# Batch 2's keys and queries by transposing DMA, later loads gated, orders new: attention in front of a two-layer MLP

## The chip, the cores and the metric

The kernel runs on one core of one Trainium2 chip. The metric is the device time of one execution in microseconds. Before the change it is 246.92 us, the median of three executions (246.78 to 246.98).

## The reference

The inputs are `q`, `k`, `v` of shape (8 batches, 8 heads, 576 tokens, 64), a packed query `p` of (8, 8, 32, 64) and two weight matrices. The attention runs twice: `p` attends to `k` and `v`, which gives 32 packed rows for each head, and `q` then attends to these rows, which are its keys and its values at once. The heads laid side by side make 4608 tokens of width 512 for an MLP with 2048 hidden units.

```python
def sm_attn(qq, kk, vv):                      # softmax over the last axis, scale 1/8
    ...
p_packed = sm_attn(p, k, v)
x = sm_attn(q, p_packed, p_packed)            # then (4608, 512)
h = x @ w_in
g = where(h >= 1, h, where(h <= -1, 0, (h + 1) ** 2 / 4))
out = g @ w_out                               # (4608, 512), float32
```

## The kernel before

**Work of one batch.** Loads by POOL's DMA queue bring k, q and v of a batch and cast them to bf16 on the way (`load`, L288). Keys and queries must be turned, so that the head dimension lies over the partitions. There are two ways, chosen in `trans` (L582) for each half (four heads) of k and of q: `by_array` (L400) turns on TensorE, twelve matmuls against an identity into a PSUM tile (`tp`, L409), which ACT or DVE copies to SBUF; `turned` (L574) issues one transposing DMA on SP's queue (L576). Batches from `TURNED` = 3 on take the DMA for all four halves; `BY_DMA` names halves of earlier batches that take it as well, before the change the second query half of batch 2.

Then follow, for each batch: the scores of the packed queries against the keys (`sp`, L436) and their exponential (`ex`, L439); the packed rows and their sums (`pk`, L456 and L462); the second scores (`s`, called s2 in the code, L490), their exponential (`eT`, L500), a matmul with a block of ones that sums and spreads them (`sm`, L505), and the division as an exponential of a logarithm (`ln` L510, `rc` L515, `A` L525). The attention output itself is never formed: the packed rows are multiplied into w_in first (`mp`, L556, copied to `M`), so that the hidden layer is `h = M * A` (L612), 16 tiles of four matmuls for a batch. Each h tile passes ACT (L617), ACT or DVE (L622 or L624) and DVE (L627), which make g, stored turned as `hT`.

**Output tiles.** Two batches are a pair of 1152 tokens and give nine output tiles of 128 tokens, 16 accumulating matmuls each (`o`, L671). A tile is copied to `ob` by ACT or DVE (L352) and stored by SP's DMA queue (L686). The first four tiles of a pair need only the pair's first batch. The first h of a batch needs all of `A`, and so both query halves.

**What sets the order.** Every piece of work is a task with engines, a cost, a key and dependences. `Plan.run` (L135) plays them through with the constants in `C` before anything is emitted, and each engine then takes its instructions in the order that this play gave. At each step an engine takes the task that can start first by the plan, and among those that can start about then the one with the lowest key. The h tiles of batch b have the keys b to b + 15/16, the output matmuls 100 and more, so that these fill what is left; the keys of the attention's units come from the table `KEYS`, one row for each batch. PSUM tiles (`W`, three; `O`, two) are rooms that a task must wait for. While fewer than three output rooms have been taken, matmuls on zeros (L745) fill TensorE's time.

Loads keep the order in which they were added: `FIRST` for batch 0, then `ORDER` (i and o are parts of w_in and w_out; the rest are k, q and v of batch 1, and p), then k, q and v of batches 2 to 7, each released when the batch two before it has used its buffer (L727 to L729). `LATE` names the parts of M of batch 0 that wait for an h tile (L733). SP's queue carries the transposes and the output stores, in the order of the plan.

For SP the plan before has two constants: a transpose holds SP for `xt` = 6.5 us and is landed `xland` = 9.0 us after that.

Of the kernel before, what the change touches and what calls it, by code (L numbers as in the profile page):

```python
# [8 lines left out]

C = dict(load=2.93, half=1.47, w_in=2.54, w_out=2.65, rest=1.25, out=3.2, p=4.3, land=1.13, xt=6.5, xland=9.0,
         tpp=0.06, tp=0.0425, sc=0.0295, pk=1.0, s2=0.245, sm=0.245, M=0.216, h=0.49, o=0.2158, switch=0.11,
         Tca=1.12, Tcd=0.75, ex=0.807, ppo=0.4, ppT=0.41, ppa=0.4, ppd=0.22, rs=0.165,
         eT=0.741, ln=0.651, rc=0.683, A=0.816, Mca=1.014, Mcd=1.223, x=0.651, ta=0.681, td=0.459, hT=0.757, oba=0.586, obd=0.69,
         array=0.2, tell=0.04, feed=0.2567, margin=0.1705, slack=0.8261, wake=1.2, warm=7.0, early=0.06759, wait=0.2014, p4=3.041, bk=0.7609)
OVER = {"ACT": 0.104, "DVE": 0.083}
NW, NO, NX, NB = 3, 2, 5, 6
DW, FILL = 256, 512
PARTS, CUT = 4, 12  # L20

ORDER = 'i0 i1 i2 k1 o0 i3 o1 o2 k0 q0 v q1 o3 p'

UNITS = "kT0 kT1 qT0 qT1 sc0 sc1 pk0 pk1 s20 s21 sm0 sm1 M0 M1 M2 M3".split()
KEYS = [
# [8 lines left out]
SPLIT = ((0, 0), (0, 1))  # L34
LATE = (2, 3)
FIRST = "k0 k1 q0 v0 v1 q10 q11"
IDENT = 3
FLOW = {"q10": 0.75, "q11": 0.75, "k1": 1.54, "q0": 1.82, "in0": 3.55, "in1": 1.89}

TURNED = 3  # L40
BY_DMA = {2: "q1"}


class Task:
# [10 lines left out]
class Plan:  # L55
# [8 lines left out]
    def __init__(self, rooms):  # L64
        self.tasks, self.now, self.mode = [], {e: 0.0 for e in self.ENGINES}, 0
        self.rooms = {nm: [0.0] * n for nm, n in rooms.items()}
        self.count = {nm: 0 for nm in rooms}
        self.now["DMA"] = 3.1
        self.log = []

    def add(self, engines, cost, key, deps, fn, takes=None, readers=0, frees=None, mode=None, slack=None, after=0.0,
# [8 lines left out]
    def ready(self, t, e):  # L80
        at = 0.0
        for d in t.deps:
            if e == "PE":
                lag = 0.0 if d.on == "PE" else C["feed"] + (C["margin"] if t.slack is None else t.slack)
            else:
                lag = C["array"] if d.on == "PE" else C["tell"]
            at = max(at, d.end + lag)
        if t.takes:
            rooms = self.rooms[t.takes]
            for j in range(len(t.readers)):  # L90
                room = rooms[(self.count[t.takes] + j) % len(rooms)]
                if room is None:
                    return None
                at = max(at, room + (C["feed"] if e == "PE" else 0.0))
        return at

    def choose(self, e, given, waiting):
# [23 lines left out]
        for c in sorted(found, key=lambda c: c[1:3]):  # L121
            if c[0] < best[0] + C["wait"] * best[3].cost[e]:
                return c[0], c[3]
# [11 lines left out]
    def run(self, idle):  # L135
        self.line = [t.seq for t in self.tasks if t.engines == ("DMA",)]
        left = {}
        given = {e: [] for e in self.ENGINES}
        for t in self.tasks:
            left[t] = len(t.deps)  # L140
            for d in t.deps:
                d.users.append(t)
            if not t.deps:
                for e in t.engines:
                    given[e].append(t)
        n, fill = len(self.tasks), 0
        while n:
            best = None
            for e in self.ENGINES:
                c = self.choose(e, given, n)  # L150
                if c is not None and (best is None or c[0] < best[0]):
                    best = c[0], e, c[1]
            if self.count["O"] < 3:
                c, step = self.choose("PE", given, n), DW / 2400
                self.now["PE"] = max(self.now["PE"], C["wake"])
                if self.now["PE"] < C["warm"]:
                    step *= 2
                if (c is None or c[0] > self.now["PE"] + step + C["early"]) and best is not None and best[0] > self.now["PE"]:
                    fill += DW
                    self.now["PE"] += step  # L160
                    continue
            assert best is not None
            at, e, t = best
            t.on = e
            cost = t.cost[e]
            if e == "PE" and at < C["warm"]:
                cost *= 2
            if e == "PE" and t.mode is not None and t.mode != self.mode:
                cost += C["switch"]
                self.mode = t.mode  # L170
            self.now[e] = at + (max(cost - OVER[e], 0.02) if e in OVER else cost)
            t.end = at + cost + t.after + (C["land"] if e == "DMA" else 0.0)
            if e == "DMA":
                del self.line[0]
            self.log.append((at, at + cost, e, t))
            if t.takes:
                room = self.rooms[t.takes]
                t.slots = [(self.count[t.takes] + j) % len(room) for j in range(len(t.readers))]
                self.count[t.takes] += len(t.slots)
                for n_, j in zip(t.readers, t.slots):  # L180
                    room[j] = None if n_ else t.end + t.holds
            if t.frees is not None:
                f, j = t.frees
                f.gone[j] = max(f.gone[j], t.end)
                f.readers[j] -= 1
                if f.readers[j] == 0:
                    self.rooms[f.takes][f.slots[j]] = f.gone[j]

            while e == "PE" and fill:
                w = min(fill, FILL)  # L190
                idle(w)
                fill -= w
            if len(t.engines) > 1:
                t.fn(e)
            elif e in ("ACT", "DVE"):
                t.fn(e)
            else:
                t.fn()
            for x in t.engines:
                given[x].remove(t)  # L200
            for u in t.users:
                left[u] -= 1
                if left[u] == 0:
                    for x in u.engines:
                        given[x].append(u)
            n -= 1
# [3 lines left out]
def kernel(  # L210
# [52 lines left out]
    PE, ACT, DVE, DMA, SP = "PE", "ACT", "DVE", "DMA", "SP"  # L263
# [42 lines left out]
    def add_load(nm, b, parts=1, deps=(), cost="load"):  # L306
        for i, hs in enumerate([ALL] if parts == 1 else HS):
            L[nm, b, i] = add(DMA, C[cost] / parts, -1, deps, lambda nm=nm, b=b, hs=hs: load(nm, b, hs))
        if parts == 1:
            L[nm, b, 1] = L[nm, b, 0]  # L310

    def add_weights(which, f):
        if which == "in":
            fn = lambda: nc.gpsimd.dma_start(w_in_sb[:, :, f * FW:(f + 1) * FW], w_in_v[:, :, f * FW:(f + 1) * FW])
        else:
            fn = lambda: nc.gpsimd.dma_start(w_out_sb[:, 4 * f:4 * f + 4], w_out_v[:, 4 * f:4 * f + 4])
        L[which, f] = add(DMA, FLOW.get(which + str(f), C["w_" + which]), -1, (), fn)

# [10 lines left out]
    for n, nm in enumerate(FIRST.split()):  # L329
        i = int(nm[1])  # L330
        L[nm[0], 0, i] = add(DMA, FLOW.get(nm, C["half"] / (len(nm) - 1)), -1, (), (lambda: None) if n else first_loads)
        for j in (range(2) if len(nm) == 2 else (int(nm[2]),)):
            part_of[nm[0], i, j] = L[nm[0], 0, i]
    for nm in ORDER.split():
        if nm == "p":
# [47 lines left out]
    K = {}  # L383
# [6 lines left out]
    def attention(b, key):  # L390
# [197 lines left out]
        q1, qc1 = trans("q", 1, qT, old("s2"))  # L588
        pk, pc, r = zip(*([packed((0,), [e0]), packed((1,), [e1])] if b == 0 or b == 1 and "v0" in ORDER else [packed((0, 1), [e0, e1])] * G))
        K[b, "sc"], K[b, "pk"] = [s0, s1], list(pk)  # L590
# [133 lines left out]
    attention(0, keys[0])  # L724
    for b in range(B):
        if b + 2 < B:
            add_load("k", b + 2, deps=K[b, "kt"])  # L727
            add_load("q", b + 2, deps=K[b, "qt"])
            add_load("v", b + 2, deps=K[b, "pk"])  # L729
        K[b, "h"] = [hidden_tile(b, fi, b + fi / KF) for fi in range(KF)]  # L730
        if b == 0:

            for f in LATE:  # L733
                K[b, "M"][f].deps.append(K[b, "h"][4 * f - 4])
            attention(1, keys[1])
            add_pT(PB, B, C["p4"], [L["p", PB]], False)
        if b % 2 == 1:
            for i in range(NT):
                out_tile(b // 2, i)
        if 0 < b < B - 1:  # L740
            attention(b + 1, keys[b + 1])
# [34 lines left out]
```

## Time and profile before

| | |
|---|---|
| time, median of three | 246.92 us |
| profiled execution | 246.60 us, of which the span from the first to the last instruction is 244.8 us |
| TensorE busy | 238.5 us (97%), its clock granted at 0.997 |
| ACT, DVE, POOL busy | 188.8, 170.4 and 30.4 us |
| software DMA queue (loads) | 18.55 MB, 53.4% of the 16 engines' time |
| SP's DMA queue (stores and transposes) | 15.70 MB, 32.7% |

A row of the profile names the line, the engine (PE is TensorE's matmul, PEld its weight load), the operation and output<-input by the program's names. `x24` is a count. In the table of slices a digit is the busy share of one fortieth of the span in tenths. In the timeline and the chain, the first number is the start in us from the span's beginning, the second the length. Times of matmuls overlap in the timeline, since matmuls are pipelined; the chain counts no time twice. A DMA's row gives the median time from its issue to its landing.

### The profile page before, as it was taken

Reading aid. Unit: us, or ns where it says so; the run is one execution under the profiler, and the core shown is the slowest. Engines: PE = TensorE matmul, PEld = TensorE weight load, DVE = VectorE, ACT = ScalarE, POOL = GpSimd, SP = SyncE. Lnnn points to the kernel's source line nnn. Section 1 sums busy time; section 2 is a strip of 40 time slices with the busy share of each in tenths; the row PEclk is TensorE's granted clock in tenths of the full one; section 3 lists DMA queues with packets and bytes.
Section 4 is the critical chain, followed back from the end, with each engine's and each line's share of the span. In section 5 each row is a group of like instructions: output and inputs, shape, how many; then the busy total and the mean of one; then the engine's idle time right before and its main releaser. Section 6 shows DMA issues by size and latency. Waiting matters only on the chain.

```text
span 244.8 us, 5431 instructions
## 1 busy us (share of the span) xinstructions
PE 238.5 (97%) x2211; PEld 137.9 (56%) x2211; DVE 170.4 (70%) x299; ACT 188.8 (77%) x314; POOL 30.4 (12%) x45
## 2 busy tenths in 40 slices
PE   7998999999999999999999999999999999999994
PEld 2645666566654764566446754675456644664443
DVE  5467994889964798369936996499669936992000
ACT  2378994889948998899888996899889957992110
POOL 8743232010110112002010200000000000000000
PEclk9999999999999999999999999999999999999998
DMA  7999999999999999999969598734170122022222
GB/s 105 198 206 205 207 203 198 202 220 204 210 211 160 245 213 165 138 202 200 208 110 236 78 160 151 162 71 92 43 137 0 46 43 70 19 43 81 54 82 86
DMA packets 55960, 34.65 MB, mean 142 GB/s; under 512 B 28672, under 2 KB 51456, under 8 KB 55936
## 3 DMA queue, kind: packets, MB, share of 16 engines
q0 software_dynamic: 24688, 18.55, 53.4%
q1 hardware_dynamic: 31104, 15.70, 32.7%
q8 instruction: 17, 0.28, 0.4%
q10 hardware_dynamic: 144, 0.07, 0.1%
q14 instruction: 7, 0.06, 0.1%
HBM read 37.22 MB, written 9.44 MB: 191 GB/s over the span
## 4 chain that ended last, share of the span: by engine, by line
PE 90%; DMA 5%; POOL 2%; issue 1%; ACT 0%; ACTq 0%; POOLq 0%
PE o L671 52%; PE h L612 26%; DMA w_in_sb<-in_moe_w_in_dram 5%; PE mp L556 3%; PE pk L456 2%; PE sp L436 2%; PE tp L409 1%; PE sm L505 1%; PE s L490 1%; PE pk L462 1%; POOL q L288 1%; PE o L745 1%; POOL v L288 1%; POOL k L288 0%; PE tpp L366 0%
## 5 line engine op out<-in xcount | busy, mean ns | idle before, releaser
L671 PE MATMUL o<-w_out_sb,hT 128*128 128x512 bf16 (+2 forms) x592 | 140.7, 374 | 0.0
L627 DVE SCALAR_TENSOR_TENSOR hT<-x 128x576 bf16<-128x576 f32 x128 | 90.2, 749 | 0.7
L671 PEld LDWEIGHTS <-hT 128*128 128x128 bf16 x592 | 55.4, 98 | 56.0 <-issue 5.0
L617 ACT ACTIVATE x<-h 128x576 f32<-128x576 f32 x128 | 75.8, 664 | 2.5 <-PE h L612 1.9
L612 PE MATMUL h<-A,M 128*128 128x288 bf16 x512 | 73.9, 286 | 0.3 <-ACT x L617 0.2
L612 PEld LDWEIGHTS <-M 128*128 128x128 bf16 x512 | 49.5, 98 | 21.0 <-issue 1.2
L622 DVE TENSOR_SCALAR x<-x 128x576 f32<-128x576 f32 x73 | 31.4, 459 | 12.5 <-ACT x L617 12.5
L624 ACT ACTIVATE x<-x 128x576 f32<-128x576 f32 x55 | 37.0, 701 | 0.1
L352 ACT COPY ob<-o 128x512 f32<-128x512 f32 (+1 forms) x24 | 14.0, 583 | 21.5 <-PE o L671 21.5
L352 DVE COPY ob<-o 128x512 f32<-128x512 f32 (+1 forms) x9 | 6.0, 670 | 25.4 <-PE o L671 25.3
L352 DVE CAST M<-mp 128x1024 bf16<-128x1024 f32 (+1 forms) x16 | 18.4, 1153 | 7.0 <-PE mp L556 5.2
L525 DVE SCALAR_TENSOR_TENSOR A<-eT,rs,rc 128x576 bf16<-128x576 bf16 (+1 forms) x15 | 11.5, 775 | 14.0 <-ACT rc L515 14.0
L352 ACT CAST M<-mp 128x1024 bf16<-128x1024 f32 (+1 forms) x18 | 16.8, 972 | 5.2 <-PE mp L556 4.8
L439 ACT ACTIVATE ex<-sp 96x768 bf16<-96x768 f32 x16 | 12.8, 807 | 4.8 <-PE sp L436 4.8
L745 PE MATMUL o<-zeros 128*128 128x512 bf16 (+1 forms) x47 | 13.7, 406 | 1.2 <-DVE zeros L276 1.2
L288 POOL DMA_DIRECT2D q<-in_q_dram x11 | 8.3, 757 | 51.6 <-DMA qT<-q 30.7
L510 ACT ACTIVATE ln<-sm 128x576 f32<-128x576 f32 (+1 forms) x17 | 10.6, 621 | 4.1 <-PE sm L505 3.9
L500 ACT ACTIVATE eT<-s,rs 128x576 bf16<-128x576 f32 (+1 forms) x17 | 11.6, 716 | 2.5 <-PE s L490 2.2
L288 POOL DMA_DIRECT2D k<-in_k_dram x10 | 7.5, 747 | 37.3 <-DMA kT<-k 24.9
L515 ACT ACTIVATE rc<-ln 128x576 f32<-128x576 f32 (+1 forms) x17 | 11.1, 655 | 0.5
L556 PE MATMUL mp<-w_in_sb,ppT 64*32 64x512 bf16 x256 | 10.7, 380 | 0.7 <-DMA w_in_sb<-in_moe_w_in_dram 0.7
L288 POOL DMA_DIRECT2D v<-in_v_dram x9 | 7.0, 775 | 16.4 <-PE pk L462 14.3
(48 smaller groups left out, 117.2 us busy)
## 6 DMA issues: line engine op xcount, KB each, us to landing
out_dram<-ob SPq DMA_DIRECT2D x23, 192.0 KB, 3.2
v<-in_v_dram POOLq DMA_DIRECT2D x7, 576.0 KB, 13.5
k<-in_k_dram POOLq DMA_DIRECT2D x6, 576.0 KB, 14.9
q<-in_q_dram POOLq DMA_DIRECT2D x6, 576.0 KB, 12.6
out_dram<-ob SPq DMA_DIRECT2D x22, 128.0 KB, 3.0
w_in_sb<-in_moe_w_in_dram POOLq DMA_DIRECT2D x4, 512.0 KB, 12.7
w_out_sb<-in_moe_w_out_dram POOLq DMA_DIRECT2D x4, 512.0 KB, 17.6
out_dram<-ob SPq DMA_DIRECT2D x22, 64.0 KB, 3.5
```

What stands on the lines that cost most here:

```text
L288: nc.gpsimd.dma_start(tok[nm, b][:, hs].rearrange("p h c d -> p h (c d)"), SRC[nm][b, hs].rearrange("h (p c) d -> p h (c d)", c=NC))
L352: return lambda eng: nc.vector.tensor_copy(out_, in_) if eng == DVE else nc.scalar.copy(out_, in_)
L439: nc.scalar.activation(ex()[:, :, i].rearrange("p e x a n -> p e (x a n)"), box["sp"], AF.Exp, scale=scale)
L500: nc.scalar.activation(box["eT"][:, xs], box["s2"][:, xs, :HALF], AF.Exp, scale=rs()[:, g, 1:])
L556: nc.tensor.matmul(mp[a * NP:(a + 1) * NP, g], pp_of(y, h), w_in_sb[y * D:(y + 1) * D, h // 2, f * FW:(f + 1) * FW], start=True, stop=True)
L612: nc.tensor.matmul(h[:, hf, :HALF], T[b, "M"][:, g, fi * P:(fi + 1) * P], T[b, "A"][:, g, hf], start=(g == 0), stop=(g == G - 1))
L617: nc.scalar.activation(box["x"], box["h"][:, :, :HALF], AF.Prelu, bias=-1.0, alpha=0.5)
L622: nc.vector.tensor_scalar(x, x, 1.0, 0.0, ALU.add, ALU.max)
L624: nc.scalar.activation(x, x, AF.Relu, bias=1.0)
L627: nc.vector.scalar_tensor_tensor(hT[:, fi, col:col + S].rearrange("p (a t) -> p a t", a=2), box["x"], 1.0, box["x"], ALU.min, ALU.mult)
L671: nc.tensor.matmul(box["o", j, part][:, :cs.stop - cs.start], hT[:, fi, i * P:(i + 1) * P], w_out_sb[:, fi, cs], start=(fi == 0 or fi in c ...
L745: plan.run(lambda w: nc.tensor.matmul(o[:, :w], zeros[:, :P], zeros[:, :w], start=True, stop=True))
```

## The change

The change has four parts.

1. `BY_DMA` names all four halves of batch 2, so that both key halves and both query halves are turned by the DMA.
2. The loads of batches 4 to 7 take one more condition, from `PACE`: those of batch b wait for the last h tile of batch b - 3 on TensorE.
3. The plan has another picture of SP's queue: a transpose begins when the one before it has had its turn, takes 6.5 us of turn if the current load ends more than 1 us later and 1.7 us otherwise, and is landed 1.8 us after its turn; a transpose beside loads and a store also push the loads back.
4. `ORDER`, `LATE`, `KEYS`, `FLOW` and several constants of the plan have new values, so that the instructions of every engine stand in a new order.

```diff
-C = dict(load=2.93, half=1.47, w_in=2.54, w_out=2.65, rest=1.25, out=3.2, p=4.3, land=1.13, xt=6.5, xland=9.0,
+C = dict(load=2.93, half=1.45, w_in=2.55, w_out=2.55, rest=1.25, out=3.2, p=4.3, land=1.13, xt=6.5, xs=1.7, xland=1.8, store=0.65,
...
-         array=0.2, tell=0.04, feed=0.2567, margin=0.1705, slack=0.8261, wake=1.2, warm=7.0, early=0.06759, wait=0.2014, p4=3.041, bk=0.7609)
+         array=0.2, tell=0.04, feed=0.1952, margin=0.1875, slack=0.5648, wake=1.2, warm=7.0, early=0.2339, wait=0.02713, p4=13.81, bk=4.48)
...
-ORDER = 'i0 i1 i2 k1 o0 i3 o1 o2 k0 q0 v q1 o3 p'
+ORDER = 'i0 i2 i1 o1 o0 i3 k1 o2 k0 q0 v q1 o3 p'
...
 KEYS = [
...
-    [2.829, 0.713, 2.940, 1.880, 2.243, 2.146, 1.163, 1.347, 1.162, 0.900, 2.620, 1.749, 1.581, 3.049, 2.830, 1.608],
...
+    [1.609, 3.246, 2.961, 2.006, 2.435, 2.926, 3.925, 3.344, 1.643, 2.402, 2.379, 3.963, 1.909, 1.610, 1.771, 4.354],
...
+PACE = {4: (1, 15), 5: (2, 15), 6: (3, 15), 7: (4, 15)}
 SPLIT = ((0, 0), (0, 1))
-LATE = (2, 3)
+LATE = (3,)
...
-FLOW = {"q10": 0.75, "q11": 0.75, "k1": 1.54, "q0": 1.82, "in0": 3.55, "in1": 1.89}
+FLOW = {"k0": 1.48, "k1": 1.52, "q0": 1.59, "v0": 1.46, "v1": 1.39, "q10": 0.75, "q11": 0.74, "in0": 3.4}
...
-BY_DMA = {2: "q1"}
+BY_DMA = {2: 'k0 k1 q0 q1'}
...
-        self.now["DMA"] = 3.1
+        self.now["DMA"], self.turn = 3.1, 0.0
...
+            if e == "SP":
+                busy, begin = self.now["DMA"] > at + 1.0, max(self.turn, at + 0.6)
+                self.turn = begin + (C["xt"] if busy else C["xs"])
+                self.now["DMA"] += C["xs"] if busy else 0.0
+                self.now[e] = max(at + C["xland"], begin)
+                cost = self.turn - at
+            if t.takes == "ob" and e != "PE" and self.now["DMA"] > at:
+                self.now["DMA"] += C["store"]
...
         if b + 2 < B:
-            add_load("k", b + 2, deps=K[b, "kt"])
-            add_load("q", b + 2, deps=K[b, "qt"])
-            add_load("v", b + 2, deps=K[b, "pk"])
+            gate = [K[PACE[b + 2][0], "h"][PACE[b + 2][1]]] if b + 2 in PACE else []
+            add_load("k", b + 2, deps=K[b, "kt"] + gate)
+            add_load("q", b + 2, deps=K[b, "qt"] + gate)
+            add_load("v", b + 2, deps=K[b, "pk"] + gate)
```

14 rows, old and new, of the table KEYS are left out of this document.

## The prediction

> **What bounds the kernel now.** I read the page's busy table first, then the table of stretches (all work, then the filler matmuls alone, then the output matmuls alone), because a share over the whole span says nothing of the one batch that the change touches most.
>
> ```profile
> span 244.8 us, 5431 instructions
> PE 238.5 (97%) x2211; PEld 137.9 (56%) x2211; DVE 170.4 (70%) x299; ACT 188.8 (77%) x314; POOL 30.4 (12%) x45
> DMA  7999999999999999999969598734170122022222
> ```
>
> TensorE is busy for 97% of the span; the DMA engines are full for the first half of the 40 slices and slack after it. Next, stretches: start:end, length, busy time and instruction count of each engine. The first fence counts everything, the second only the filler (L745), the third only the output matmuls (L671).
>
> ```profile
> 30.00:79.54 49.54, 49.52 (x530) 28.96 (x528) 38.63 (x62) 40.03 (x64) 7.05 (x9) 1.00 1.32 201
> 79.54:241.40 161.86, 161.86 (x1394) 93.83 (x1392) 111.98 (x189) 129.65 (x219) 7.21 (x9) 1.00 0.69 117
> ```
>
> ```profile
> 19.58:30.00 10.42, 1.86 (x7) 0.58 (x6) 1.00 1.25 206
> ```
>
> ```profile
> 0.00:79.54 79.54, 33.40 (x131) 11.99 (x131) 1.00 1.26 195
> ```
>
> From 30.00 to 241.40 us TensorE is busy 211.38 of 211.40 us. So the end moves only by work taken off TensorE, by waits put into it, and by what happens before 30 us. The profiled execution took 246.60 us, 1.8 us over its span and 0.32 us under the median of 246.92. Both terms below are differences, so I add them to the median.
>
> **The change part by part.** *The transposes of batch 2.* Before, both key halves and one query half go over TensorE (L409); one query half goes by DMA (L576). The chain of work shows start and length:
>
> ```profile
> 47.91 1.02 PE tp L409 x24
> 50.48 0.55 PE tp L409 x12
> ```
>
> All three groups leave the full engine: 1.02 + 0.55 = **1.57 us off**. Their evictions leave ACT and DVE, which had 9.51 and 10.91 us of the stretch 30.00:79.54 free (49.54 less 40.03 and 38.63): worth 0, since TensorE, not they, fills that stretch.
>
> *What is late next.* Three transposes join one in SP's queue. SP's timeline (start, how long SP was held), then the time from issue to landing of those four transposes in order, and of a lone one issued at 153.13 us:
>
> ```profile
> 50.37 1.84 SPq L576 DMA_TRANSPOSE qT<-q  x1
> 52.48 5.47 SPq L686 DMA_DIRECT2D out_dram<-ob  x4
> 58.13 3.24 SPq L576 DMA_TRANSPOSE kT<-k  x1
> 62.88 6.05 SPq L576 DMA_TRANSPOSE kT<-k  x1
> 69.05 6.67 SPq L576 DMA_TRANSPOSE qT<-q  x1
> ```
>
> ```profile
> qT<-q SPq DMA_TRANSPOSE x1, 10.8
> kT<-k SPq DMA_TRANSPOSE x1, 12.9
> kT<-k SPq DMA_TRANSPOSE x1, 16.7
> qT<-q SPq DMA_TRANSPOSE x1, 13.0
> qT<-q SPq DMA_TRANSPOSE x1, 3.5
> ```
>
> They landed at 61.2, 71.0, 79.6 and 82.0 us: 10.8 to 16.7 us each beside loads, against 3.5 alone. The packets of 66 to 68 us (two queues) and of 154.4 to 156.0 us (SP's alone) tell why:
>
> ```profile
> q0 software_dynamic: 375, 0.28, 90.3%
> q1 hardware_dynamic: 376, 0.10, 36.3%
> ```
>
> ```profile
> q1 hardware_dynamic: 1149, 0.29, 101.0%
> ```
>
> Beside loads the queues advance packet for packet, 376 of SP's in 2 us; alone, a transpose's 1149 packets pass in 1.6 us. Beside loads one needs 1149 / 188 = 6.1 us, and SP's stores share that queue.
>
> When do batch 2's four land? The load of its keys, by issue on POOL and time to landing:
>
> ```profile
> 31.28 0.78 POOL L288 DMA_DIRECT2D k<-in_k_dram  x1 [1.74 <-DMA w_out_sb<-in_moe_w_out_dram]
> ```
>
> ```profile
> k<-in_k_dram POOLq DMA_DIRECT2D x1, 576.0 KB, 16.1
> ```
>
> Keys land at 47.4, so the first transpose at 47.4 + 10.8 = 58.2. At the old spacing, (82.0 - 61.2) / 3 = 6.9 us, the fourth lands at 79. At SP's 6.05 us for two more and 2 us for a last one without loads, it lands at 72. I take **75**: keys of batch 4 now wait for batch 2's landed keys (some 65 us) and then fill the queue again beside the last two, though with fewer loads behind them than before.
>
> Need: both query halves feed s2 (L490), whose chain (eT, sm, ln, rc, A) ends in the first h of batch 2. The chain of work:
>
> ```profile
> 69.74 0.37 PE s L490 x16
> ...
> 72.41 0.35 PE sp L436 x12
> ...
> 73.00 3.45 PE o L671 x16
> ...
> 79.70 1.47 PE h L612 x12
> ...
> 149.80 0.37 PE s L490 x16
> ...
> 156.51 0.98 PE h L612 x8
> ```
>
> From s2 to h took 9.96 us here, 6.7 two batches later; I take 6.7. The cover for a late h is output work of the first pair: 9 tiles of 16 matmuls are 144, of which 131 ran before 79.54, so 13 x 3.45/16 = 2.8 us remain. TensorE runs out of work at 79.70 + 2.8 - 1.57 - 0.35 (the scores of batch 3, at 72.41, whose keys now land behind batch 2's) = 80.6. With the fourth half landed at 75, s2 runs at 75.3 and h at 82.0: a wait of **1.4 us**, the least it can be. It grows if the written order puts s2 earlier, since TensorE then stands at s2 with the outputs behind it. The planner's new rule (6.5 us a busy transpose, 1.7 one that it takes for idle, 1.8 to land) puts the fourth at 47.4 + 0.6 + 4 x 6.5 + 1.8 = 75.8 if it counts all as busy, at 71.0 with one idle, at 66.2 with two. With one idle, s2 stands at 71.4 and the wait is 75.3 - 71.4 = 3.9. I take the middle of 1.4 and 3.9, **+2.65 us**; the ends are 0 (landing by 73.6) and 5.6 (two idle, s2 at 69.7 as before).
>
> *Gates.* Loads of batches 4 to 7 wait in POOL's queue for the last h of batches 1 to 4; behind them stand only the other loads of the same batch. For batch 5 the last h of batch 2 and its own first scores, from the chain, and its keys' time from issue to landing:
>
> ```profile
> 92.27 0.51 PE h L612 x4
> ...
> 130.18 0.35 PE sp L436 x12
> ```
>
> ```profile
> k<-in_k_dram POOLq DMA_DIRECT2D x1, 576.0 KB, 10.3
> ```
>
> 92.27 + 0.51 + 10.3 + at worst 16.7 = 119.8, 10 us before 130.2: cost 0, and without that cover each us late would be a us. The gain, quieter transposes, comes after 65 us, too late for batch 2's first two. For batch 4 the landed keys of batch 2 are the later condition, so that gate hardly binds; I price it at 0 (ends -1 and +1, the share of one 2 us packet window).
>
> *Orders.* w_out part 0 comes behind part 1 and ahead of batch 1's k1: by the planner's own costs 2.55 - 1.45 = 1.1 us later, where 1.86 us of filler already ran (19.58:30.00). Against it, M of part 2 no longer waits for an h, and k1's transposes leave this stretch. Ends +1.1 and -1.1; I take 0, also because time won there only lengthens the wait at batch 2. The transposes of p (key 3.04 to 13.81) and the first pair's copies (key -0.24 to 3.48) may fall behind h of batch 1; I take 0, as the wait for batch 2 covers a shift of 1 or 2 us.
>
> Sum: 246.92 - 1.57 + 2.65 = **248.0**.
>
> **The rivals.** *A, the transposes land in time (faster).* Place: s2 of batch 2; it decides at a landing of 73.6. No wait, 246.92 - 1.57 = 245.35. For it: the last of the four quoted landed only 2.4 us after the third; the gates thin the loads. Against: 6.1 us of packets each. In a sentence of its own: the Trainium skill, "DMA: Bandwidth & Descriptors", section "Anatomy of one DMA", fits about 2.0 us plus bytes over 436 GB/s (for the software path), an estimate of 2.7 us for 0.29 MB, and by it all four would land near 58 and this rival would hold. The trace disagrees with that figure in this stretch: 10.8 to 16.7 us.
>
> *B, only the uncovered part counts.* The order is written late enough and 1.4 us is all: 246.92 - 1.57 + 1.4 = 246.75, no change. For it: the planner knows of the busy queue. Against: its 1.8 us from turn to landing, where 58.13 to 71.0 lies behind a predecessor landed at 61.2.
>
> *C, TensorE stands at s2 for 5.6 us*: 250.95. For it: TensorE takes its queue in order (it runs the rows of the chain one behind the other), and the rule may count two transposes as idle. Against: the four would then be planned less than 19 us after the keys.
>
> *D, the change does not do what it says*: the gate is idle and the loads run as before; the fourth lands at 79, h at 79.3 + 6.7 = 86.0, wait 5.4, 250.75. It goes with C.
>
> **How the numbers follow.** Forecast (247.3 to 249.3) 0.40; A 0.35; B 0.13; C and D 0.12. About 0.2%, 0.5 us, is what a measurement of this kernel tells from no change. Faster: A and a quarter of B, 0.38. Within: half of B, 0.07. Slower: the rest, 0.55. The range 245.0 to 250.0 takes in A, whose startup end could reach 244.3, and the forecast, and leaves out C and D and A's tail, under 2 in 10.
>
> **What would show it.** Right: no L409 rows after batch 1; four transposes for batch 2 with the last landing at 73 to 78; a TensorE gap of 1 to 4 us between 63 and 82 us put down to qT or kT; dense TensorE afterwards; k of batch 5 issued after the last h of batch 2. Wrong: TensorE without a gap there (A), a gap before 40 us put down to w_out or to k1, or waits at the scores of batches 4 to 7, which would mean that the gates cost.

## The result, and the profile after

| | before | after |
|---|---|---|
| median | 246.74 us (246.3 to 246.98, six runs) | 250.48 us (248.99 to 251.83, six runs) |
| profiled execution, its span | 246.60 us, 244.8 us | 248.99 us, 247.2 us |

The ratio is 1.0155, with an interval of 1.0114 to 1.0195: slower by 1.1 to 2.0%. The prediction had 248.0 us and a range that ended at 250.0. Where some executions of a kernel took over 1.5% longer than its shortest (one of four of e3_q1_only, three of six of e11_told_and_gated), its median and ratio below are those of the others alone.

The first lines of the page after, the counterparts of those shown before:

```profile
span 247.2 us, 5318 instructions
PE 234.6 (95%) x2127; PEld 135.4 (55%) x2163; DVE 172.6 (70%) x306; ACT 181.9 (74%) x304; POOL 30.5 (12%) x45
DMA  7999999999999999999999999922220121122222
```

The DMA engines are full for 25 of the 40 slices, from the second to the 26th, where before the first dip came in slice 21. TensorE's 234.6 us are too low: 559 output matmuls are recorded where there are 592 weight loads (L680), so 33 records of them are missing. I therefore read its waits from the timeline. The stretches of the same profile (start:end, length, then busy time and count of PE, PEld, DVE, ACT, POOL, granted clock, DMA share, GB/s), and after them the transposing matmuls alone (L418), up to 63 us and behind it:

```profile
63.00:81.73 18.73, 15.66 (x175) 7.80 (x177) 9.65 (x16) 11.87 (x19) 3.08 (x4) 1.00 1.27 201
81.73:95.00 13.27, 12.18 (x120) 8.72 (x121) 11.40 (x23) 12.89 (x23) 0.00 (x0) 1.00 1.29 197
```

```profile
0.00:63.00 63.00, 6.09 (x96) 4.86 (x96) 1.00 1.24 193
63.00:247.00 184.00, 0.00 (x0) 0.00 (x0) 1.00 0.75 127
```

The 96 are those of batches 0 and 1 (for each, four halves of twelve), so the transposing matmuls of batch 2 are gone. TensorE's time is lost between 63 and 95 us. Its timeline there names the places (start, length, then in brackets the idle time before the row and what ended it); the last row is the weight load of the row above it:

```profile
62.77 0.81 PE L680 MATMUL o<-w_out_sb,hT 128*128 128x512 bf16 x3
65.20 0.52 PE L445 MATMUL sp<-pT,kT 128*128 128x64 bf16 x12 [1.62 <-DMA kT<-k]
...
70.66 2.55 PE L680 MATMUL o<-w_out_sb,hT 128*128 128x512 bf16 x11
74.06 0.44 PE L499 MATMUL s<-qT,ppT 64*32 64x288 bf16 x16 [0.84 <-DMA qT<-q]
...
74.87 1.03 PE L680 MATMUL o<-w_out_sb,hT 128*128 128x512 bf16 x4 [0.16 <-issue]
76.22 0.52 PE L445 MATMUL sp<-pT,kT 128*128 128x64 bf16 x12 [0.32 <-DMA kT<-k]
...
81.73 1.15 PE L621 MATMUL h<-A,M 128*128 128x288 bf16 x8
...
93.44 0.38 PE L680 MATMUL o<-w_out_sb,hT 128*128 128x512 bf16 x1
94.81 0.53 PE L445 MATMUL sp<-pT,kT 128*128 128x64 bf16 x12 [0.99 <-ACT x L633]
94.81 0.41 PEld L445 LDWEIGHTS <-kT 128*128 128x128 bf16 x12 [1.39 <-DMA kT<-k]
```

Four waits for a transpose: the scores of batch 2, s2 of batch 2, the scores of batch 3 and the scores of batch 4. At the last of them the matmul's bracket names ACT, but its weight load's names kT, and the key half of batch 4 lands at 94.76, 0.05 us before the row. An output matmul is drawn 0.38 long, while sixteen of them take 3.45 us (the prediction's chain), 0.216 each; from the end by that step to the next row the four waits are 65.20 - 63.42 = 1.78, 74.06 - 73.03 = 1.03, 76.22 - 75.73 = 0.49 and 94.81 - 93.66 = 1.15 us, together **4.45**. With the 1.57 us taken off, that makes +2.88 where the two profiled executions differ by 248.99 - 246.60 = 2.39. Of the missing -0.5 us, 0.3 lies behind the last matmul: from the start of the last copy of an output tile to the end of the span it is 244.8 - 241.50 = 3.3 us before and 247.2 - 244.22 = 3.0 after. The other 0.2 I did not find in a place of its own.

SP's timeline of the same kernel, then the time from issue to landing of its rows at 57.90 and 65.45 us, and, from the chain of waits, of the second transpose of the first row and of the first key half of batch 3:

```profile
47.53 7.88 SPq L585 DMA_TRANSPOSE kT<-k  x2
...
57.90 6.41 SPq L585 DMA_TRANSPOSE qT<-q  x1
...
65.45 2.81 SPq L585 DMA_TRANSPOSE qT<-q  x1
...
83.28 6.23 SPq L585 DMA_TRANSPOSE kT<-k  x1
```

```profile
qT<-q SPq DMA_TRANSPOSE x1, 11.2
```

```profile
qT<-q SPq DMA_TRANSPOSE x1, 8.6
```

```profile
49.34 15.81 DMA kT<-k
...
68.36 7.81 DMA kT<-k
```

The second key half of batch 2 lands at 65.15, its query halves at 69.1 and 74.0, the first key half of batch 3 at 76.17, that of batch 4 at 94.8 (11.5 us after its issue). The packets of 57 to 60 us show the sharing again, one for one:

```profile
q0 software_dynamic: 572, 0.43, 92.0%
q1 hardware_dynamic: 573, 0.14, 37.1%
```

The Trainium skill, "DMA: Bandwidth & Descriptors", section "Queues, rings and completion order", says that each DMA engine takes the queues in turn, packet by packet. The trace agrees.

Last, POOL's queue, with the issue of k of batch 4 and k of batch 5:

```profile
65.73 0.77 POOL L297 DMA_DIRECT2D k<-in_k_dram  x1 [22.32 <-DMA kT<-k]
...
79.23 0.77 POOL L297 DMA_DIRECT2D k<-in_k_dram  x1 [2.51 <-DMA kT<-k]
```

The change's text says that k of batch 5 waits for the last h of batch 2. It is issued at 79.23, before the *first* h of batch 2 (81.73). Its bracket names what it did wait for: the transposed keys of batch 3, landed at 78.65. **The gates are not carried out on the chip.** `PACE` puts an h tile into the dependences of a task of the plan. The plan then counts on the load being late, but the DMA that is emitted has no operand in common with that h tile, so no instruction waits for it. The loads ran free beside the transposes of batches 3 and 4.

What the plan counted on can be had from the plan's own play, which needs no chip (half kT1 is the second key half by number, qT0 the first query half):

```
half            landing in the plan   landing in the trace   its reader in the plan   and in the trace
kT1, batch 2    62.76                 65.15                  64.66                    65.20
qT0, batch 2    66.16                 74.01                  72.86                    74.06
kT1, batch 3    72.66                 76.17                  74.87                    76.22
kT1, batch 4    82.56                 94.76                  92.24                    94.81
k of batch 5    issued at 92.22       issued at 79.23
```

Each reader that the plan had put 2 to 10 us behind the landing came ahead of it on the chip, and TensorE, which takes its instructions in order, stood.

### The profile page after: what moved, and what is told of

Read it like the earlier page. It is cut to its first block, busy times and chain, and to the rows that moved or that the text cites. A ratio compares the mean times of both kernels' runs of the same rounds, so it can differ in the third digit from the quotient of the medians.

```text
span 247.2 us, 5318 instructions
## 1 busy us (share of the span) xinstructions
PE 234.6 (95%) x2127; PEld 135.4 (55%) x2163; DVE 172.6 (70%) x306; ACT 181.9 (74%) x304; POOL 30.5 (12%) x45
## 4 chain that ended last, share of the span: by engine, by line
PE 63%; DMA 21%; DVE 6%; ACT 3%; issue 2%; POOL 2%; ACTq 0%; POOLq 0%
PE o L680 40%; PE h L621 13%; DMA kT<-k 10%; DMA q<-in_q_dram 7%; DMA w_in_sb<-in_moe_w_in_dram 5%; DVE hT L636 4%; PE mp L565 3%; ACT x L626 2%; PE pk L465 2%; DVE x L631 2%; PE sp L445 2%; PE sm L514 1%; ACT x L633 1%; PE s L499 1%; POOL q L297 1%
## 5 line engine op out<-in xcount | busy, mean ns | idle before, releaser
L680 PE MATMUL o<-w_out_sb,hT 128*128 128x512 bf16 (+2 forms) x559 | 134.9, 373 | 1.7 <-issue 0.3
L680 PEld LDWEIGHTS <-hT 128*128 128x128 bf16 x592 | 54.7, 98 | 55.2 <-issue 5.0
L626 ACT ACTIVATE x<-h 128x576 f32<-128x576 f32 x128 | 76.8, 669 | 7.2 <-PE h L621 6.7
L631 DVE TENSOR_SCALAR x<-x 128x576 f32<-128x576 f32 x77 | 32.9, 458 | 11.9 <-ACT x L626 11.9
L633 ACT ACTIVATE x<-x 128x576 f32<-128x576 f32 x51 | 35.2, 703 | 0.1
L361 DVE CAST M<-mp 128x1024 bf16<-128x1024 f32 (+1 forms) x16 | 18.9, 1188 | 7.3 <-PE mp L565 7.0
L509 ACT ACTIVATE eT<-s,rs 128x576 bf16<-128x576 f32 (+1 forms) x17 | 11.4, 717 | 6.1 <-PE s L499 6.1
L448 ACT ACTIVATE ex<-sp 96x768 bf16<-96x768 f32 x16 | 12.7, 812 | 4.2 <-PE sp L445 4.1
L755 PE MATMUL o<-zeros 128*128 128x512 bf16 (+1 forms) x32 | 10.1, 436 | 1.4 <-DVE zeros L285 1.2
L445 PE MATMUL sp<-pT,kT 128*128 128x64 bf16 x192 | 8.2, 193 | 2.9 <-DMA kT<-k 1.9
## 6 DMA issues: line engine op xcount, KB each, us to landing
w_in_sb<-in_moe_w_in_dram POOLq DMA_DIRECT2D x4, 512.0 KB, 12.7
```

Of the source, the lines that this page charges most:

```text
L361: return lambda eng: nc.vector.tensor_copy(out_, in_) if eng == DVE else nc.scalar.copy(out_, in_)
L445: nc.tensor.matmul(o[:, :, a], kT()[:, i, w:w + P], pT[:, b, h], start=True, stop=True)
L448: nc.scalar.activation(ex()[:, :, i].rearrange("p e x a n -> p e (x a n)"), box["sp"], AF.Exp, scale=scale)
L626: nc.scalar.activation(box["x"], box["h"][:, :, :HALF], AF.Prelu, bias=-1.0, alpha=0.5)
L631: nc.vector.tensor_scalar(x, x, 1.0, 0.0, ALU.add, ALU.max)
L633: nc.scalar.activation(x, x, AF.Relu, bias=1.0)
```

## The experiments

All start from the kernel after. My theory after the result was: the waits come because transposes land later than the plan has them, beside loads that the plan holds back and the chip does not. The rivals were that the transposes of batch 2 by DMA cost the time whatever the plan says, and that the new orders cost it. Kernels that were measured together share the runs of the kernel before, whose median lay between 246.97 and 247.11 us.

### The same kernel again (a0_after)

> The changed kernel once more, for a second profile and for its spread (248.99 to 251.83 us in six executions, where the kernel before keeps within 0.7). Theory: the spread is TensorE's waits for transposes, whose landing varies; a slower execution shows longer waits for kT and qT between 63 and 100 us and nowhere else. Rival: the spread lies elsewhere (longer instructions, stores, the start).

No edit. 250.14 us (249.38 to 251.22), ratio 1.0128 (1.0091 to 1.0164). Its profiled execution took 250.03 us, 1.04 more than the one above, and its timeline says where most of that is:

```profile
75.14 0.44 PE L499 MATMUL s<-qT,ppT 64*32 64x288 bf16 x16 [1.80 <-DMA qT<-q]
```

The scores of batches 2 and 3 wait as above (1.43 and 0.24 in their rows), and s2 waits 0.96 us more, since the query half came at 75.09 instead of 74.01. The four waits come again; by the step used above they are 1.59, 1.96, 0.40 and 1.18, together 5.13 us. That is 0.7 more than above, of the 1.04 between the two executions. For the spread of the other executions, which have no profile, this is not shown.

### Gates that hold (e2_real_gates)

```diff
+        if nm == "k" and b in PACE:
+            gb, gf = [w for w in emitted if w[0] == PACE[b][0]][-1]
+            mark = const.tile([P, 1], bf16, name="mark" + str(b))
+            nc.gpsimd.tensor_copy(mark, hT[:, gf, (gb % 2) * S:(gb % 2) * S + 1])
...
+            emitted.append((b, fi))
```

POOL copies one column of the last hT tile before it issues the load of k, so its queue really waits (`emitted` lists the h tiles in the order in which their last step is written).

> Same orders as the changed kernel; only the keys' loads of batches 4 to 7 now really wait on POOL (a one-column copy out of the hidden tiles), where in the changed kernel nothing on the chip held them. Theory (transposes land later than the written order assumes, because loads run beside them): the waits at batch 2 (scores at 65.2, s2 at 74.1 us, together some 2.8 us) stay, since batch 3's loads are untouched; the wait at the scores of batch 4 (1.2 us at 94.8) goes. Time some 249.0, 1 to 1.5 us under the changed kernel's 250.5. Rival (missing gates are innocent): 250.5 within 0.5. Rival (gates held for real starve batches 4 to 7): above 251.5, with waits for k, kT or v after 100 us.

249.55 us, ratio 1.0115 (1.0040 to 1.0189). k of batch 5 is issued at 99.45 instead of 79.23, the key half of batch 4 lands at 89.5, and the wait at batch 4's scores is gone. s2 no longer waits either. The two others stay:

```profile
65.39 0.52 PE L449 MATMUL sp<-pT,kT 128*128 128x64 bf16 x12 [1.52 <-DMA kT<-k]
...
76.72 0.52 PE L449 MATMUL sp<-pT,kT 128*128 128x64 bf16 x12 [1.54 <-DMA kT<-k]
```

So the free loads made the wait at batch 4, but holding them does not restore the time: batch 3's scores take over 1.2 us of it. As times the two kernels aren't told apart (the intervals overlap), so the places decide here: the theory had the scores of batches 2 and 4 right, s2 and the scores of batch 3 not.

### No gates in the plan (e1_plan_ungated)

```diff
-PACE = {4: (1, 15), 5: (2, 15), 6: (3, 15), 7: (4, 15)}
+PACE = {}
```

> The changed kernel without PACE: the planner no longer believes that batches 4 to 7 load late, which on the chip they did not. Theory: orders up to 92 us are the same, so the waits at 65, 74 and 76 us stay, and batch 4's scores still stand in the order before its transposes land; some 250, within 1 us of the changed kernel. Rival (the planned gates are most of the loss): 248 or less.

267.26 us, ratio 1.0782 (1.0738 to 1.0826); theory and rival both missed by far. The orders up to 92 us are the same, and the waits stand at the same places (1.70, 1.80 and 0.51 us in their rows). Behind them stand two new ones, at the keys of batch 5 and at a query half:

```profile
115.75 0.82 PE L445 MATMUL sp<-pT,kT 128*128 128x64 bf16 x12 [7.15 <-DMA kT<-k]
...
145.10 0.68 PE L499 MATMUL s<-qT,ppT 64*32 64x288 bf16 x16 [6.14 <-DMA qT<-q]
```

A plan that knows the loads to be free is no better, as long as its picture of a transpose beside loads is wrong: it put the scores of batch 5 at 104.44, behind keys that it had at 103.76 and that landed at 115.70. The planned gates alone don't explain the loss.

### One transpose of batch 2, with the new plan (e3_q1_only)

```diff
-BY_DMA = {2: 'k0 k1 q0 q1'}
+BY_DMA = {2: "q1"}
```

> The changed kernel with one query half of batch 2 alone on the DMA, as before the change; the planner writes its orders anew from the same keys and constants. Theory: three transposes return to TensorE (+1.57 us) and the wait for batch 2 goes (-2.8 us or more); the loads that run past the planned gates still delay batch 4's scores: 247 to 249. Rival (orders and the new picture of SP's queue are the cause, not batch 2's transposes): 250 or more.

255.35 us, ratio 1.0322 (1.0256 to 1.0387): here the theory missed and the rival held. The profiled execution was the kernel's longest, 258.57 us, so its waits are upper ends:

```profile
73.79 0.82 PE L445 MATMUL sp<-pT,kT 128*128 128x64 bf16 x12 [3.15 <-DMA kT<-k]
...
105.85 0.52 PE L445 MATMUL sp<-pT,kT 128*128 128x64 bf16 x12 [2.65 <-DMA kT<-k]
```

With the transposes of batch 2 back as they were before, the scores of batches 3 and 4 wait: the plan had the first at 69.2, behind keys that it had at 68.7 and that landed at 73.74. So the new picture of SP's queue (part 3 of the change) with its orders puts readers ahead of landings by itself; the three moved transposes are not needed for it. The keys of the order were not chosen for this kernel, so its loss is no measure of their share in the loss of the kernel after.

### Quiet transposes for batch 2 (e8_load3_waits, e9_both_waits, g8_load3_waits_keys, g9_both)

Which load stands beside them? k of batch 3, and behind it the rest of that batch. In e8, POOL first copies a few columns of batch 2's turned halves, so that this load waits for them; e9 adds the gates of e2.

```diff
+        if nm == "k" and b == 3:
+            mark = const.tile([P, 3], bf16, name="turned")
+            nc.gpsimd.tensor_copy(mark[:, :2], kTs[0][:, :, 0])
+            nc.gpsimd.tensor_copy(mark[:, 2:], qTs[0][:, 1, :1])
```

> Same orders as the changed kernel; only the load of batch 3's keys, and the loads queued behind it on POOL, wait until both key halves and the first query half of batch 2 have landed. Theory (loads beside the transposes make them late): with the DMA engines free of loads from about 55 us, both key halves land before 61 and the query halves before 67 us; no TensorE wait for kT or qT of batch 2; batch 3's scores may wait up to 1 us; time 246.5 to 248.5. Rival (the written order is at fault whatever the DMA does): the h tiles of batch 2 still start at 81 us or later and the time stays at 250.5. Rival (later loads of batch 3 cost as much as they give): waits move to the scores of batch 3 and 4, time 250 or more.

> Both real waits together: batch 3's loads behind batch 2's transposes, and the gates of batches 4 to 7 held on the chip; orders as in the changed kernel. Theory: no TensorE wait for a transpose of more than 0.5 us anywhere, so that the 1.57 us taken off TensorE show: 245.0 to 246.5, under the kernel before. Rival (the new orders themselves cost): over 247.5 without such waits.

259.77 us, ratio 1.0497 (1.0445 to 1.0549), and 259.71 us, ratio 1.0492 (1.0438 to 1.0545). In e8 the four halves of batch 2 landed at 56.0, 57.0, 61.1 and 63.8 us and nothing of batch 2 waited: the contention is what makes them late, as the theory said. The time went to batch 3, as the last rival of e8 said. In e9, where the theory saw no wait anywhere, the same place waits 11.99 us. POOL's timeline of e8, then TensorE's:

```profile
61.23 6.52 POOL L300 COPY turned<-qT 128x1 bf16<-128x1 bf16 x1 [3.35 <-DMA qT<-q]
67.68 0.77 POOL L301 DMA_DIRECT2D k<-in_k_dram  x1
```

```profile
85.57 0.82 PE L449 MATMUL sp<-pT,kT 128*128 128x64 bf16 x12 [11.86 <-DMA kT<-k]
```

A copy of one column took 6.52 us, k of batch 3 left at 67.68, its first turned half landed at 85.5, and TensorE stood for 11.86 us. Since the copy spoils the measurement, g8 and g9 hold the load with a small DMA instead, and for the two key halves only:

```diff
+        if nm == "k" and b == 3:
+            mark = const.tile([P, 2, 64], bf16, name="turned")
+            nc.gpsimd.dma_start(mark[:16], kTs[0][:16, :, :64])
```

> Orders of the changed kernel; batch 3's keys' load waits on POOL, by a small DMA in place of the copy, for batch 2's two key halves only. Theory: batch 2's key halves land by 58 us and its query halves by 69, so that the waits at 65 and 74 us go; batch 3's loads run 5 us later than in the changed kernel and its scores wait 0 to 4 us: 247 to 250. Rival: what batch 2 gains batch 3 loses in full, 250.5 or more.

> As the run before it, and the gates of batches 4 to 7 held on the chip by the same kind of small DMA. Theory: loads of batch 5 no longer run beside the transposes of batch 4, so the wait there goes as well: 0.5 to 1.5 us under the run before it, 246 to 249. Rival: no difference between the two.

256.34 us, ratio 1.0364 (1.0342 to 1.0387), and 255.97 us, ratio 1.0359 (1.0336 to 1.0381). In g8 the load left at 58.49, the key halves of batch 2 landed at 56.3 and 57.3, and:

```profile
73.72 0.44 PE L502 MATMUL s<-qT,ppT 64*32 64x288 bf16 x16 [1.51 <-DMA qT<-q]
...
81.90 0.82 PE L448 MATMUL sp<-pT,kT 128*128 128x64 bf16 x12 [6.33 <-DMA kT<-k]
```

What batch 2 gains, batch 3 loses several times over: the rival of g8 held. g9 is not told apart from g8, so its rival held too. In none of these four kernels did it pay to keep the loads of batch 3 away from the transposes of batch 2; whether another place for the hold would is not shown.

### The plan told when transposes land (e10_plan_told, e11_told_and_gated)

e10 changes no load and no transpose. It only adds to the plan's landings the lateness that the trace after shows, eleven values of 2.4 to 12.2 us:

```diff
+LAG = {(2, "k", 0): 2.6, (2, "k", 1): 2.4, (2, "q", 1): 4.7, (2, "q", 0): 7.9, (3, "k", 1): 3.5, (3, "q", 1): 10.2,
+       (3, "q", 0): 6.7, (4, "k", 1): 12.2, (4, "k", 0): 3.1, (4, "q", 1): 10.9, (4, "q", 0): 10.3}
...
-            t = add(SP, C["xt"], key[nm + "T" + str(i)], [L[nm, b, i]] + prev, go, after=C["xland"])
+            t = add(SP, C["xt"], key[nm + "T" + str(i)], [L[nm, b, i]] + prev, go, after=C["xland"] + LAG.get((b, nm, i), 0.0))
```

> The planner is told the landings that the changed kernel's profile showed (2.4 to 12.2 us later for the transposes of batches 2 to 4), and writes the orders with these; nothing else changes. Theory: what the changed kernel loses is that the written order puts scores and s2 before their transposes land; written later, only what no output work covers stays, and the 1.57 us come off: 246.5 to 248. Rival (transposes beside loads cost whatever the order is): 249.5 or more, with waits for kT or qT of over 1 us again.

248.57 us, ratio 1.0061 (1.0040 to 1.0083), 1.57 us under the same kernel without the knowledge, run beside it (250.14); the ranges of theory and rival both missed it. Of the wait at batch 2's scores 0.59 us is left (0.43 in its row), batch 3's is gone, and at batch 4's no TensorE row waits for keys any more. The one at s2 remains, since the half that the plan was told for 74.06 came at 75.69 this time:

```profile
75.73 0.44 PE L502 MATMUL s<-qT,ppT 64*32 64x288 bf16 x16 [2.19 <-DMA qT<-q]
```

So the plan's optimism makes about half of the loss (1.57 of 250.14 - 247.11 = 3.03). The other half stays with a landing that this order does not cover: h of batch 2 comes at 83.71. Whether another order would cover it is not shown.

e11 does both, knowledge (from the landings of e2) and loads really held by small DMAs: k of batch 4 behind the query halves of batch 2, k of batches 5 to 7 behind their h tiles.

```diff
+        if nm == "k" and b == 4:
+            mark = const.tile([P, 2, 64], bf16, name="turned")
+            nc.gpsimd.dma_start(mark[:16], qTs[0][:16, :, :64])
+        if nm == "k" and b in PACE and b > 4:
+            gb, gf = [w for w in emitted if w[0] == PACE[b][0]][-1]
+            mark = const.tile([P, 64], bf16, name="mark" + str(b))
+            nc.gpsimd.dma_start(mark[:16], hT[:16, gf, (gb % 2) * S:(gb % 2) * S + 64])
...
```

> Two things on top of the changed kernel: the planner is told the landings that the run with real gates showed (1.0 to 6.9 us later for the transposes of batches 2 to 4), and the gates are held on the chip by small DMAs on POOL, the one of batch 4 behind batch 2's query halves. Theory: the fourth transpose lands near 71.4, TensorE waits under 1 us in all for transposes, and the h tiles of batch 2 start at 80.5 to 82: 246 to 247.3, no slower than the kernel before by more than 0.2%. Rival (orders cost by themselves): 248 or more without such waits. Rival (waits return elsewhere): 248 or more with them.

255.58 us (253.99 to 256.16; the other three took 259.10 to 260.41), ratio 1.0326 (1.0293 to 1.0359): the theory missed, and the rival with waits elsewhere held. Up to h of batch 2, at 80.17, it is better than e10. Then the held load of batch 5 is let go at 92.96, right beside a key half of batch 4 issued at 94.15, which lands at 108.49 where the plan has 95.6. The profiled execution, again the longest of its kernel:

```profile
108.53 0.82 PE L454 MATMUL sp<-pT,kT 128*128 128x64 bf16 x12 [9.62 <-DMA kT<-k]
```

Here, as in e8, the hold moved the collision to where it ended.

### One transpose fewer, told and held (e13_k1q_told, e14_k1q_unheld)

e13 leaves the first key half of batch 2 on TensorE, has a table of landings of its own and the holds of e11:

```diff
-BY_DMA = {2: 'k0 k1 q0 q1'}
+BY_DMA = {2: 'k1 q0 q1'}
+
+LAG = {(2, 'k', 1): 2.9, (2, 'q', 1): 7.3, (2, 'q', 0): 5.1, (3, 'k', 1): 3.2, (3, 'k', 0): 1.0, (3, 'q', 1): 3.0, (3, 'q', 0): 4.5}
...
```

e14 is e13 without the small DMAs that hold the loads, with the same plan and the same orders.

> As the run before it, but one key half of batch 2 (k0) goes back to TensorE: three transposes for batch 2 in place of four, so that the last lands some 5 us earlier, near 69.6, before the work that covers it runs out at about 80.5 less 6.7. Theory: the 0.5 us of work given back buys the whole wait at s2: 245.8 to 247. Rival: the last query half lands after 72 all the same, 247.5 or more.

> The run with three transposes for batch 2 and told landings, with every order as there, but without the small DMAs on POOL that held the loads of batches 4 to 7. Theory: the keys of batch 4, which then load from about 65 us, and those of batch 5, from about 80, run beside transposes again; waits of 1 to 4 us at s2 of batch 2 and at the scores of batch 4: 247 to 250. Rival (the later orders alone did it): 245.6 within 0.5.

e13: **245.59 us** (245.41 to 245.70) against 247.09, ratio **0.9934** (0.9920 to 0.9947): faster than both kernels, and 0.2 us under the theory's range. e14: 247.16 us against 246.97, ratio 1.0007 (0.9995 to 1.0019). POOL's and TensorE's timelines of e13 (k of batches 4 and 5, then s2 and the first h of batch 2):

```profile
70.89 0.79 POOL L306 DMA_DIRECT2D k<-in_k_dram  x1
...
92.37 0.78 POOL L306 DMA_DIRECT2D k<-in_k_dram  x1
```

```profile
72.16 0.44 PE L508 MATMUL s<-qT,ppT 64*32 64x288 bf16 x16
...
79.34 0.65 PE L630 MATMUL h<-A,M 128*128 128x288 bf16 x4
```

And of e14, POOL's and TensorE's:

```profile
59.60 0.77 POOL L299 DMA_DIRECT2D k<-in_k_dram  x1 [16.04 <-PE h L623]
```

```profile
73.30 0.44 PE L501 MATMUL s<-qT,ppT 64*32 64x288 bf16 x16 [1.18 <-DMA qT<-q]
```

In e13, k of batch 4 leaves at 70.89, just after the last query half of batch 2 landed (69.55), and no TensorE row waits for a kT or qT. In e14 the same load leaves at 59.60, the query half issued at 57.86 lands at 73.25, and s2 waits (a weight load's wait of 0.33 for kT, at 74.97, comes with no idle time of TensorE). The holds are worth 247.16 - 245.59 = 1.57 us by the medians and 246.59 - 245.46 = 1.13 by the two profiled executions; e14's wait at s2 is 1.18 + 0.16 = 1.34. The theory's second place, the scores of batch 4, did not wait. This is the cleanest test of the mechanism: same orders, same transposes, and only whether a load waits is different. The hold of k of batch 5 does not end clear of all transposes here either: let go at 92.37, the load runs beside a query half issued at 95.76, which took 12.33 us. But the plan had that half's reader only at 127.14, while in e11 it had the scores that read the late key half at 97.91. Of e13's 1.5 us under the kernel before, the two groups of matmuls taken off explain 2/3 of 1.57 = 1.05, and 0.3 lies behind the last matmul, as above (243.7 - 240.69 = 3.0); the rest has no place that I found.

## Why the prediction was wrong, point by point

*Transposing matmuls off, -1.57: right.* No such row stands after batch 1.

*Landings in batch 2: right within a microsecond.* First 58.2 forecast, 47.53 + 11.4 = 58.9 seen; fourth 75 forecast, 74.0 and 75.1 seen in two profiles; k of batch 4 into the queue at some 65, seen at 65.73; first h at 82.0, seen at 81.73. That h is right because two errors cancel, which is luck: the half landed 1.0 us sooner than 75, and from s2 to h it took 81.73 - 74.06 = 7.67 us where I had taken 6.7. The mechanism, transposes that share packets with loads and TensorE standing in order, is the one that the traces show.

*The wait, +2.65 at s2 alone: this is the step that failed.* I priced one place, and put the waits at the scores of batches 2, 3 and 4 at nothing without a reason. Measured were 4.45 us in four: 1.78 at the scores of batch 2, 1.03 at s2, 0.49 at the scores of batch 3, 1.15 at those of batch 4; in the second profile 5.13, of which 1.96 at s2. Batch 2's two together, 2.81, are near my term, but that is luck, since the term was for s2 alone. I treated the key halves as if an early landing of the first were all that mattered: the scores need the second, at 65.15; the plan had them at 64.66, and TensorE was there at 63.42. And I took the middle between "one transpose counted as idle" and none; the plan counted two, its landing of the fourth half was the 66.2 that I had worked out for that case, 7.9 us early. It cost no more than this at s2 because the plan put s2 at 72.86, 6.7 us behind that landing. The profiled execution is the shortest of the six; the median stands 1.49 us over it, and for that part there is only the second profile.

*Gates, 0: wrong in kind.* I priced them as waits that are carried out, with 10 us of cover for batch 5. Nothing waited. The cost came from the opposite side: a plan that counts on quiet, 12.2 us early for batch 4's key half, beside a load that was not held. My sign "waits at the scores of batches 4 to 7, which would mean that the gates cost" appeared, and its reading was the reverse; e2 shows it, since with real gates that key half lands at 89.5 and the wait goes. The sign that would have told, k of batch 5 issued after the last h of batch 2, failed. Reading how a dependence in the plan becomes a wait in the program would have shown it beforehand. The 10 us of cover were not there either: I read them from the old order, and the changed kernel runs the first scores of batch 5 at 119.70, where my sum for their keys ended at 119.8.

*Orders, 0 with ends of ±1.1: held within its ends for the start, which is what I priced.* Of the -0.5 us left over in the sum 0.3 lies behind the last matmul, so some -0.2 is left for it. What the orders do behind 63 us I had put into the term for s2 alone; e10 shows that this was mis-sized: orders written with the seen landings take 1.57 us off.

*Rivals.* A and B fell. D's premise, a gate that is idle and loads that run as before, is what the trace shows, with C's rule of two idle transposes; their 250.75 and 250.95 lie beside the measured 250.48, but by luck, since both drew all of it at s2, where 1.03 and 1.96 us were seen. I had given them 0.12 together, arguing that four landings within 19 us of the keys would not be planned. They were: 66.16 - 47.36 = 18.8 in the plan.

*What stays open.* 0.2 of the -0.5 us, and why the span's end is 0.3 shorter; the waits of the executions without a profile; why e11's and e13's tables, each made from other kernels' landings, fit so differently well after 90 us; and whether four transposes in batch 2 can be paid at all. With told landings they cost 248.57, with one on TensorE and real holds 245.59.

## What to carry to other kernels

A dependence that stands only in a host-side plan holds nothing on the chip: look for the instruction that waits, and in the trace for what ended the wait of the transfer that should be late. Where an engine takes its queue in order, a plan that is too hopeful about a landing costs, at each reader, what its own slack does not cover: 7.9 us too hopeful cost 1.03 at s2, behind 6.7 of slack, and 2.4 cost 1.78 at the scores of batch 2, where TensorE also came 1.2 us sooner than planned. Move only as many transposes to the DMA as land under cover, and hold the loads beside them with a real wait that ends where the readers of the transposes then under way are still far off.

## What the runs showed of the hardware that was not expected

*A GpSimd copy beside a busy VectorE.* The copy of one column (128 elements) took 0.19 us at one place of e2 and 5.47 at another:

```profile
68.19 0.19 POOL L300 COPY mark<-hT 128x1 bf16<-128x1 bf16 x1 [24.48 <-DVE hT L641]
...
94.04 5.47 POOL L300 COPY mark<-hT 128x1 bf16<-128x1 bf16 x1 [19.96 <-DVE hT L641]
```

VectorE's rows beside the long one, and the row that follows:

```profile
93.90 0.82 DVE L635 TENSOR_SCALAR x<-x 128x576 f32<-128x576 f32 x2
94.63 2.09 DVE L641 SCALAR_TENSOR_TENSOR hT<-x 128x576 bf16<-128x576 f32 x3
96.64 0.82 DVE L635 TENSOR_SCALAR x<-x 128x576 f32<-128x576 f32 x2
97.38 2.08 DVE L641 SCALAR_TENSOR_TENSOR hT<-x 128x576 bf16<-128x576 f32 x3
99.38 1.22 DVE L365 CAST M<-mp 128x1024 bf16<-128x1024 f32 x1
```

VectorE ran these two kinds without a pause until 99.46, and the copy ended at 99.51, when VectorE turned to an operand in PSUM. Beside the short copy, at 68.19, such a run had just ended (67.36 + 0.76 = 68.12). The 6.52 us of e8 end at 67.75, where such a run of VectorE ends at 67.70. The Trainium skill, "SBUF — State Buffer", section "SBUF: two separate sides", says that VectorE, in some modes or with two SBUF inputs, and GpSimd exclude each other on a shared pair of ports for a whole instruction. The runs agree that they exclude each other, but not with one instruction's length: the copy lost to about ten in a row.

*The clock after a long wait.* Stretches of e8, columns as above; TensorE stands from 73.7 to 85.57:

```profile
78.00:80.00 2.00, 0.00 (x0) 0.00 (x0) 0.00 (x0) 0.00 (x0) 0.00 (x0) 0.50 1.30 184
90.00:92.00 2.00, 2.00 (x8) 0.79 (x7) 0.82 (x1) 0.52 (x1) 0.00 (x0) 0.78 1.23 257
86.00:120.00 34.00, 34.00 (x340) 19.26 (x338) 23.43 (x41) 27.09 (x43) 3.46 (x5) 0.93 1.29 207
```

The granted clock was 1.00 until 76 us, 0.81 from 76 to 78 and 0.50 from there until 90, and 1.00 again from 92. So it was halved at some 77.2, 3.5 us into the idle time, and came back at some 90.9, 5.3 us after work began again (estimates from the shares of 0.81 and 0.78). It was 0.93 over the 34 us behind the wait, which is 34 x 0.07 = 2.4 us more. With -1.57 and +11.86 that gives +12.7, and 12.78 was measured (259.77 - 246.99). The profiled executions whose waits were at most 2.2 us by their brackets had a mean clock of 1.00 (after, a0, e2, e10, e13, e14); with a longest wait of 3.15 us, in e3, it was 0.98. The Trainium skill, "TensorE: Matmul & The Clock Gate", section "Part 1: The HAM clock gate (the "warmup" mystery)", has the clock halved after an idle window of about 3.4 us; the runs agree.
